# Two of four centring quarters moved from VectorE to GpSimd in the start of a fused transformer block

## The chip, the core and the metric

The kernel runs on one core of a Trainium2 chip. The metric is the device time of one execution in microseconds (us). The time before the change is 691.56 us, the median of 3 runs (691.15 to 691.78).

## What is computed

One pre-norm transformer block over 2048 rows of 1024 columns in bf16: layer norm, sliding-window attention (32 heads of 32 columns, each query sees itself and the 255 keys before it), an output product and a residual, then a second layer norm and a dense part with SiLU, with a second residual. Cut to what matters:

```python
def _layernorm(x, axis=-1, eps=1e-5):
    m = jnp.mean(x, axis=axis, keepdims=True)
    v = jnp.var(x, axis=axis, keepdims=True)
    return (x - m) / jnp.sqrt(v + eps)

x = A_x
h = x + _A_ref(_layernorm(x, axis=-1), A_wqkv, A_wo)
h2 = h + _B_ref(_layernorm(h, axis=-1), B_w1, B_w2)
```

`_A_ref` multiplies by `wqkv` (1024 x 3072), does the windowed softmax attention and multiplies by `wo`. `_B_ref` multiplies by `w1` (1024 x 3584), applies SiLU and multiplies by `w2`.

## The kernel before

The 2048 rows are worked in four blocks of 512 rows, and a block in four row tiles of 128 rows, the number of partitions. For each block the kernel normalises the rows, transposes them (TensorE needs the 1024 columns on the partitions), and forms v, q and k; attention of a block is woven between the products of the next block. The output product and the dense part follow. The scheduling is by hand: every engine runs its instructions in the order in which the program writes them, and semaphores make one engine wait for another.

The change lies in the start, before any of this is in full swing. The very first products (v of row tiles 0 and 1) do not wait for a finished layer norm. Each of the two tiles is only centred, transposed and multiplied; the factor one over the standard deviation is applied to the product later. The order of work for tile j is:

- `half_mean(j, 1, nc.scalar)` (L467): ScalarE sums columns 512 to 1023, scaled by -1/1024, into a column of `mean`. `half_mean(j, 0, nc.vector)` (L469): VectorE does the same for columns 0 to 511, by an instruction that also writes its accumulator.
- `center(j)` (L474): four quarters of 256 columns each, `x_mid = x_ring + mean half + mean half`, bf16 in SBUF to bf16 in SBUF.
- `turn_first(j, h, ...)` (L224, L227): TensorE transposes the two 128-column pieces of quarter h into a PSUM bank, and ScalarE (or VectorE, for the last two quarters of tile 1) copies them to `lnT_b[0]`.
- products (L497) with the first 512 columns of the v weights, accumulated over the eight 128-column pieces of the tile.

TensorE's order is a list written by hand, in which a pair (j, h) is a transposition of quarter h of tile j, and a triple (j, k0, k1) are the products over pieces k0 to k1 - 1:

```python
ORDER = [
    (0, 0), (0, 1), (0, 2), (0, 0, 2), (0, 3), (0, 2, 4), (1, 0), (0, 4, 6), (1, 1), (1, 2), (1, 3), (1, 0, 4),
    (1, 4, 6), (0, 6, 8), (1, 6, 8),
]
```

Ahead of it, TensorE runs a few matmuls on zeros in float32 (`busy`, L173) while the first row tile is on its way from memory. After it come the products of the second half of the v columns (L515), the transposes of row tile 2 (L519) and the rest of v (L249), then q and k (L259).

GpSimd's work in the start is to build the identity matrix for the transposes and to set the ones column of `v` (L167, a memset). Later it does the selects of the attention mask (L382). Its instruction order and that of VectorE are those of the program. The normalisation of whole row tiles in later blocks is one VectorE tensor_scalar over 128x1024 (L208); `norm_first` (L485) is the same for tiles 0 and 1, in place, ahead of their transposition by DMA (L212).

Of the kernel before, what the change touches and what calls it, by code (L numbers as in the profile page):

```python
# [12 lines left out]
ALU = mybir.AluOpType  # L13
# [35 lines left out]
def kernel(  # L49
# [10 lines left out]
    nc = tc.nc  # L60
# [400 lines left out]
    mean = small.tile([P, 6], F32, name="mean")  # L461
# [9 lines left out]
    def center(j):  # L471
        for h in range(4):
            out, in0 = (x[j][:, h * 256:(h + 1) * 256] for x in (x_mid, x_ring))
            nc.vector.tensor_scalar(out=out, in0=in0, scalar1=mean[:, j * 2:j * 2 + 1], scalar2=mean[:, j * 2 + 1:j * 2 + 2], op0=ALU.add, op1=ALU.add)  # L474

    acc_banks += [o[:].rearrange("p a b -> p (a b)") for o in o_ps]
    def var_first(j):
# [9 lines left out]
    for j in range(2):  # L487
        half_mean(j, 1, nc.scalar)
        half_mean(j, 0, nc.vector)
        center(j)  # L490
    nc.vector.tensor_tensor(out=mean[:, 4:6], in0=mean[:, 0:4:2], in1=mean[:, 1:4:2], op=ALU.add)
    first = [next_acc() for _ in range(2)]
    for step in ORDER:
        if len(step) == 3:
            j, k0, k1 = step
# [193 lines left out]
    for b in range(NB):  # L689
# [4 lines left out]
        for ft in range(FT):  # L694
# [8 lines left out]
            if b == 0 and 7 <= ft < 15:  # L703
                j, c = divmod(ft - 7, 2)
# [60 lines left out]
```

## Time and profile before

| What | us |
|---|---|
| median of 3 runs | 691.56 (691.15 to 691.78) |
| span of the profiled execution, first to last instruction | 690.4 |
| busy in the span: TensorE | 676.3 (98%) |
| VectorE | 292.3 (42%) |
| ScalarE | 244.5 (35%) |
| GpSimd | 161.1 (23%) |
| first row tile landed, first half mean starts | 4.03 |
| first transposition | 5.24 |

The profiled execution has no time of its own beside its span; the median of the runs is 1.2 us above the span. In the profile PE is TensorE, PEld its weight loads, DVE is VectorE, ACT is ScalarE, POOL is GpSimd, SP is SyncE, which issues most DMAs. L474 is line 474 of the kernel. A line of the timeline gives start, length, engine, line, operation, output, input, shapes and a count; instructions of one kind that follow each other are merged into one line. A pair of square brackets at the end gives the engine's idle time before it and what ended it. Ends of matmuls are modelled, their starts are recorded.

### The profile page before, as it was taken

Reading aid. Unit: us, or ns where it says so; the run is one execution under the profiler, and the core shown is the slowest. Engines: PE = TensorE matmul, PEld = TensorE weight load, DVE = VectorE, ACT = ScalarE, POOL = GpSimd, SP = SyncE. Lnnn points to the kernel's source line nnn. Section 1 sums busy time; section 2 is a strip of 40 time slices with the busy share of each in tenths; the row PEclk is TensorE's granted clock in tenths of the full one; section 3 lists DMA queues with packets and bytes.
Section 4 is the critical chain, followed back from the end, with each engine's and each line's share of the span. In section 5 each row is a group of like instructions: output and inputs, shape, how many; then the busy total and the mean of one; then the engine's idle time right before and its main releaser. Section 6 shows DMA issues by size and latency. Waiting matters only on the chain.

```text
span 690.4 us, 14117 instructions
## 1 busy us (share of the span) xinstructions
PE 676.3 (98%) x5890; PEld 342.2 (50%) x6004; DVE 292.3 (42%) x613; ACT 244.5 (35%) x466; POOL 161.1 (23%) x295
## 2 busy tenths in 40 slices
PE   8999999999999999999999999999999999999998
PEld 4445555555555555544444444444444444444445
DVE  5167646744444458443316133343133251333111
ACT  6326666666676667421310033300133100233000
POOL 1007666666666656500000000000000000000000
PEclk9999999999999999999999999999999999999999
DMA  7933142137240888970023310022300124100110
GB/s 249 283 40 93 32 74 75 22 62 188 73 131 17 247 257 248 230 266 32 32 85 108 91 39 0 1 91 70 85 0 1 20 92 94 39 1 1 30 39 24
DMA packets 78640, 61.48 MB, mean 89 GB/s; under 512 B 52464, under 2 KB 62704, under 8 KB 78576
## 3 DMA queue, kind: packets, MB, share of 16 engines
q1 hardware_dynamic: 78432, 60.31, 32.2%
q8 instruction: 47, 0.77, 0.5%
q10 hardware_dynamic: 144, 0.26, 0.1%
q14 instruction: 17, 0.14, 0.1%
HBM read 39.85 MB, written 8.39 MB: 70 GB/s over the span
## 4 chain that ended last, share of the span: by engine, by line
PE 97%; issue 1%; DMA 0%; DVE 0%; DVEq 0%
PE hacc L675 19%; PE acc L259 16%; PE hacc L712 14%; PE acc L712 14%; PE acc L675 9%; PE acc L280 7%; PE acc L249 6%; PE o_ps L392 5%; PE sc L312 3%; PE hacc L280 1%; PE sc L364 1%; PE sc L338 1%; PE o_ps L249 1%; DMA r_o<-in_A_x_dram 0%; PE acc L497 0%
## 5 line engine op out<-in xcount | busy, mean ns | idle before, releaser
L382 POOL TENSOR_SCALAR_AFFINE_SELECT r_e<-r_e 128x512 bf16<-128x512 bf16 (+1 forms) x288 | 158.2, 564 | 124.8 <-ACT r_e L372 61.9
L712 PEld LDWEIGHTS <-r_a 128*128 128x128 bf16 x952 | 90.9, 98 | 103.0
L675 PEld LDWEIGHTS <-r_w 128*128 128x128 bf16 x896 | 87.3, 98 | 105.1 <-issue 0.5
L675 PE MATMUL hacc<-r_e,r_w 128*128 128x512 bf16 x468 | 104.9, 379 | 0.5
L712 PE MATMUL hacc<-r_a 128*128 128x512 bf16 (+1 forms) x496 | 100.2, 361 | 0.4
L324 ACT ACTIVATE r_e<-sc 128x768 bf16<-128x768 f32 x96 | 78.2, 814 | 47.9 <-PE sc L312 47.9
L712 PE MATMUL acc<-r_a 128*128 128x512 bf16 (+1 forms) x439 | 94.5, 372 | 0.5
L684 ACT ACTIVATE r_n<-hacc 128x512 f32<-128x512 f32 x30 | 17.9, 597 | 178.9 <-PE hacc L675 177.8
L259 PEld LDWEIGHTS <-r_w 128*128 128x128 bf16 x512 | 47.1, 98 | 55.0 <-issue 1.0
L261 DVE CAST r_a<-acc 128x512 bf16<-128x512 f32 x56 | 38.7, 692 | 57.0 <-PE acc L259 54.4
L259 PE MATMUL acc<-r_t,r_w 128*128 128x512 bf16 x233 | 56.5, 380 | 2.4 <-issue 1.7
L259 PE MATMUL acc<-r_w 128*128 128x512 bf16 x240 | 56.0, 379 | 1.5 <-issue 0.9
L392 PEld LDWEIGHTS <-r_e 128*128 128x128 bf16 x1440 | 47.4, 96 | 17.9
L392 PE MATMUL o_ps<-r_a,r_e 128*128 128x33 bf16 x1440 | 48.1, 178 | 0.0
L280 PE MATMUL acc<-r_o,r_a 128*128 128x512 bf16 x188 | 46.2, 380 | 1.9 <-issue 1.1
L675 PE MATMUL acc<-r_e,r_w 128*128 128x512 bf16 x191 | 43.3, 379 | 0.2
L727 DVE SCALAR_TENSOR_TENSOR r_t<-acc,r_t 128x512 bf16<-128x512 f32 (+1 forms) x16 | 10.6, 665 | 69.3 <-PE acc L712 69.3
L325 ACT ACTIVATE r_e<-sc 128x256 bf16<-128x256 f32 x96 | 37.5, 390 | 0.0
L280 PEld LDWEIGHTS <-r_a 128*128 128x128 bf16 x256 | 23.4, 98 | 26.9
L685 DVE SCALAR_TENSOR_TENSOR r_a<-r_n,hacc 128x512 bf16<-128x512 f32 x30 | 20.6, 688 | 33.0 <-ACT r_n L684 33.0
L685 DVE SCALAR_TENSOR_TENSOR r_a<-r_a,hacc 128x512 bf16<-128x512 f32 x30 | 20.6, 688 | 31.2 <-ACT r_a L684 31.2
L727 DVE SCALAR_TENSOR_TENSOR r_t<-hacc,r_t 128x512 bf16<-128x512 f32 (+1 forms) x18 | 11.6, 647 | 51.2 <-PE hacc L712 51.2
(103 smaller groups left out, 549.2 us busy)
## 6 DMA issues: line engine op xcount, KB each, us to landing
r_w<-in_B_w_dram SPq DMA_DIRECT2D x8, 896.0 KB, 5.2
r_a<-in_B_w_dram SPq DMA_DIRECT2D x7, 1024.0 KB, 7.5
r_w<-in_A_wqkv_dram SPq DMA_DIRECT2D x4, 1024.0 KB, 9.3
h_dram<-r_t SPq DMA_DIRECT2D x16, 256.0 KB, 2.8
r_t<-h_dram SPq DMA_DIRECT2D x16, 256.0 KB, 2.9
out_dram<-r_t SPq DMA_DIRECT2D x31, 128.0 KB, 1.7
r_o<-in_A_x_dram SPq DMA_DIRECT2D x15, 256.0 KB, 4.4
r_e<-h_dram SPq DMA_DIRECT2D x3, 1024.0 KB, 5.8
```

Of the source, the lines that this page charges most:

```text
L249: nc.tensor.matmul(acc, lhsT=lnT_b[b % 2][:, kt, j * P:(j + 1) * P], rhs=wv[:, kt, c * 512:(c + 1) * 512], start=(kt == 0), stop=(kt == KT ...
L259: nc.tensor.matmul(acc, lhsT=wqk[:, kt, col0:col0 + P], rhs=lnT_b[b % 2][:, kt, :], start=(kt == 0), stop=(kt == KT - 1))
L261: copy(out=(qT, kT)[which][b][:, g, :], in_=acc)
L280: nc.tensor.matmul(acc, lhsT=qT[b][:, g, j * P:(j + 1) * P], rhs=wo[:, g, c * 512:(c + 1) * 512], start=(g == 0), stop=(g == G - 1))
L324: nc.scalar.activation(out=tri[:, :, :, 64:256], in_=both, func=ACT.Exp, scale=scale)
L325: nc.scalar.activation(out=e[:, 1024:1280].rearrange("p (h q) -> p h q", q=P), in_=bank[:, :, 192:320], func=ACT.Exp, scale=scale)
L382: nc.gpsimd.affine_select(out=dst, in_=src, pattern=[[0, n] for n in dst.shape[1:-1]] + [[sgn, P]], compare_op=ALU.is_ge if upper else ALU ...
L392: nc.tensor.matmul(o_ps[pair][:, qt * 2 + hh, 0:VW], lhsT=chunk_of(i, bank, piece, pair, hh), rhs=v[:, b * 4 + kt, g * 4 + pair * 2 + hh, ...
L675: nc.tensor.matmul(acc, lhsT=w1[:, kt, ft * P:(ft + 1) * P], rhs=ln2T[b][:, kt, :], start=(kt == 0), stop=(kt == KT - 1))
L685: nc.vector.scalar_tensor_tensor(out=gT[:, ft, :], in0=th, scalar=1.0, in1=acc, op0=ALU.add, op1=ALU.mult)
L712: nc.tensor.matmul(acc[:, 0:c1 - c0], lhsT=gT[:, ft, j * P:(j + 1) * P], rhs=w2[ft // 4][:, ft % 4, c0:c1], start=(ft == 0), stop=(ft == F ...
L727: nc.vector.scalar_tensor_tensor(out=t_out[j % 2][:, c0:c1], in0=acc[:, 0:c1 - c0], scalar=0.5, in1=t_in[j % 2][:, c0:c1], op0=ALU.mult, o ...
```

## The change

The third and fourth quarter of row tile 0 (columns 512 to 1023) are centred by GpSimd instead of VectorE. The other two quarters of tile 0 and all four of tile 1 stay on VectorE, and so does everything else.

```diff
     def center(j):
         for h in range(4):
             out, in0 = (x[j][:, h * 256:(h + 1) * 256] for x in (x_mid, x_ring))
-            nc.vector.tensor_scalar(out=out, in0=in0, scalar1=mean[:, j * 2:j * 2 + 1], scalar2=mean[:, j * 2 + 1:j * 2 + 2], op0=ALU.add, op1=ALU.add)
+            engine = nc.gpsimd if j == 0 and h > 1 else nc.vector
+            engine.tensor_scalar(out=out, in0=in0, scalar1=mean[:, j * 2:j * 2 + 1], scalar2=mean[:, j * 2 + 1:j * 2 + 2], op0=ALU.add, op1=ALU.add)
```

On VectorE the half mean of tile 1 (L469) then follows right behind the second quarter of tile 0. On GpSimd the two quarters stand between the memset of `v` and the first select, behind a wait for the row tile and both half means. TensorE's transposes of quarters 2 and 3 wait for GpSimd instead of VectorE.

## The prediction

> **What bounds the kernel now.** I read the busy times of the page first, then the chain of waits for the first 13 us (the change lies there), then the timeline of single stretches to get single instructions.
>
> Page, parts 1 and 4:
>
> ```profile
> PE 676.3 (98%) x5890; PEld 342.2 (50%) x6004; DVE 292.3 (42%) x613; ACT 244.5 (35%) x466; POOL 161.1 (23%) x295
> PE 97%; issue 1%; DMA 0%; DVE 0%; DVEq 0%
> ```
>
> TensorE is busy for 98% of the span and is 97% of the chain that ended last. Whatever happens to VectorE or GpSimd counts only as far as it moves TensorE. The chain in order of time (start, length, what):
>
> ```profile
> 4.03 0.71 DVE r_e L469 x2
> ...
> 4.84 0.36 DVE r_e L474
> 5.20 0.05 issue
> 5.24 0.91 PE tp L224 x6
> 6.15 0.88 PE acc L497 x2
> 7.03 0.21 PE tp L224 x2
> 7.24 0.85 PE acc L497 x2
> 8.10 0.21 PE tp L224 x2
> 8.31 0.68 PE acc L497 x2
> 8.99 0.33 PE tp L224 x6
> 9.32 1.29 PE o_ps L497 x6
> ```
>
> Up to 5.24 us the chain is VectorE's: half mean of row tile 0, then only its first centring quarter. From there it is TensorE without a hole. So quarters 1 to 3 of tile 0, the mean of tile 1 and the centring of tile 1 are off the path already. The same lines show TensorE's clock: two 512-column matmuls take 0.85 us (0.43 each) at 7.24 and six take 1.29 us (0.215 each) from 9.32. It runs at half rate until some 8.7 us, 3.45 us after 5.24 (the pair at 8.31 takes 0.68, one at each rate).
>
> Timeline of the stretch itself (start, length, engine, line, what, idle before):
>
> ```profile
> 4.56 0.19 ACT L467 ACTIVATION_READ_ACCUMULATOR r_e<-r_o 128x1 f32 x1
> 4.84 1.11 DVE L474 TENSOR_SCALAR r_e<-r_o,mean 128x256 bf16<-128x256 bf16 x4
> 5.24 0.91 PE L224 MATMUL tp<-ident,r_e 128*128 128x128 bf16 x6 [0.77 <-DVE r_e L474]
> 5.86 0.68 DVE L469 TENSOR_SCALAR_CACHE_REDUCE r_e<-r_o 128x512 bf16<-128x512 bf16 x1
> 6.66 1.11 DVE L474 TENSOR_SCALAR r_e<-r_o,mean 128x256 bf16<-128x256 bf16 x4
> 1.31 2.32 POOL L167 MEMSET r_a<- 128x512 bf16 x1
> ```
>
> GpSimd is free from 3.63 us. The quarters start 0.257 us apart on VectorE (4.84, 5.10, 5.35, 5.61), and narrow stretches of the timeline put the transposes that need them at 5.24, 5.49, 5.75 and 6.82. The last was ready at about 6.0, so the fourth quarter has 0.8 us to spare; the third has none that shows. The first product matmul starts at 6.00, held by ScalarE's copy of quarter 0 (5.67 to 5.94).
>
> **The change, part by part.** Program order is unchanged on TensorE; the transposes of quarters 2 and 3 now wait for GpSimd. Added waits elsewhere (the in-place normalisation of tile 0 at 15.55 us, one exponential, one load of x on SP's queue) are for work done by about 6 us: nothing behind them is delayed, so nothing. No DMA is moved.
>
> VectorE loses two quarters, 2 x 0.257 = 0.51 us. The second half mean (L469) and tile 1's centring could start that much earlier. On the path this is worth nothing: TensorE takes tile 1's first transpose at 7.89, behind matmuls that follow each other without a hole, and its quarter was ready at about 7.0. So the gain is nil; what is left is what GpSimd costs.
>
> When GpSimd starts: it waits for both half means, the later being ScalarE's accumulator at 4.75. A select of GpSimd that waited for ScalarE started 0.07 us after it (51.12 to 51.19). That gives 4.82, just ahead of VectorE's first quarter at 4.84.
>
> How long a quarter takes there: the trace has no tensor_scalar on GpSimd. The nearest row is the affine select of the same engine and size, SBUF to SBUF, at 413 ns, back to back every 0.36 us; the farthest is the strided memset at L167, 2320 ns for 512 elements, 1.16 us for 256. I take the select.
>
> Do the two engines hinder each other? Rows of the next block's normalisation show it (VectorE tensor_scalar 128x1024, alone and with selects running):
>
> ```profile
> 47.32 0.54 DVE L208 TENSOR_SCALAR r_o<-r_o,st_a,rs_a 128x1024 bf16<-128x1024 bf16 x1
> 75.70 0.76 DVE L208 TENSOR_SCALAR r_o<-r_o,st_a,rs_a 128x1024 bf16<-128x1024 bf16 x1
> 75.77 0.41 POOL L382 TENSOR_SCALAR_AFFINE_SELECT r_e<-r_e 128x256 bf16<-128x256 bf16 x1
> 76.13 0.59 POOL L382 TENSOR_SCALAR_AFFINE_SELECT r_e<-r_e 128x256 bf16<-128x256 bf16 x1
> 133.58 0.99 DVE L208 TENSOR_SCALAR r_o<-r_o,st_a,rs_a 128x1024 bf16<-128x1024 bf16 x1
> 133.66 0.64 POOL L382 TENSOR_SCALAR_AFFINE_SELECT r_e<-r_e 128x512 bf16<-128x512 bf16 x1 [0.57 <-ACT r_e L324]
> ```
>
> A select that starts 0.07 us after VectorE's instruction runs undisturbed (0.41) and VectorE takes 0.22 longer; the next one is itself held up by 0.18. The longer select of 0.64 costs VectorE 0.45. So they take turns, and GpSimd gets in first even when it starts slightly later. From 75.70: delay of VectorE = 0.15 + (start of GpSimd - start of VectorE), not below nothing.
>
> Quarter 0 (VectorE 4.84, GpSimd 4.82): 0.15 - 0.02 = 0.13 late, so the first transpose at 5.37. Quarter 1: VectorE issues it at 5.10 + 0.13 = 5.23; GpSimd's second quarter starts at 4.82 + 0.36 = 5.18, delay 0.15 - 0.05 = 0.10. It is 0.23 late in all, its transposes at 5.72. Quarter 2 is ready on GpSimd by 5.23 and no longer waits for VectorE: its two transposes follow at 5.72 + 2 x 0.107 = 5.94 (half-rate pace of 128 columns, from 0.43 for 512) and end their turn at 6.15. The first product matmul is then at 6.15 instead of 6.00: TensorE loses **0.16 us**. Quarter 3 is ready at about 5.6, needed at 7.0.
>
> If GpSimd holds the way longer than the select does by e, quarter 0 pays e and quarter 1 pays it twice: loss 0.16 + 2e. [...] With the memset's rate e = (4.53 - 0.9) x 256 = 0.93 us (0.9 ns an element from 413 and 640 ns of the two sizes of select), and the loss is 2.0. The lower end: if GpSimd starts 0.1 us later, VectorE's quarter 0 goes first and the loss is about 0. Below nothing it can't go, since the matmul at 6.00 hangs on quarter 0 and ScalarE.
>
> What a loss d before 8.7 us costs at the end: half-rate time is lost. If the clock turns at the same moment, the missing work is done later at double pace, d/2; if the turn moves by d too, d. All later work hangs on TensorE, with no slack that takes it up. Sum: 0.08 to 0.16 us at the value taken, up to 0.4 with e = 0.13. I forecast **+0.2 us**. The profiled execution spans 690.4 us, and the median of the runs is 691.56; I take the 1.2 us around the span as unchanged. That gives a span of 690.6 and a time of **691.8 us**. About 0.2% (1.4 us) is what a measurement of this kernel can tell from no change, so this is "same".
>
> **The rivals.** *The clock turns a whole stretch later (slower).* TensorE was busy with its first matmuls from 1.12 to 4.48 and stayed at half rate; after 0.77 us of idling, 3.45 us of unbroken work raised it. If a new hole at 5.35 to 5.75 spoils this stretch, another such stretch passes at half rate: it costs (3.45 + 0.16) / 2 = 1.8 us, 693.4 us. It decides as soon as the holes exceed what the rise tolerates; the idle 0.77 did not pass, the present 0.1 us between pairs of transposes does. Against it: my holes sum to some 0.3 us, spread out. [...] Chance 0.23.
>
> *GpSimd is slow at this operation (slower).* With the memset's rate, quarter 0 is 0.13 + 0.93 late and TensorE loses 2.0 us. Nothing raises the clock earlier, since work starts later: +1.0 to 2.0, up to 693.6 us. It ends slower from e = 0.6 us. For it: no row shows this operation; against it: the memset's elements lie 66 bytes apart, the quarters' are adjacent. Chance 0.11.
>
> *The freed VectorE pays (faster).* Were a wait of TensorE hidden in the chain, the whole of its idle time between 5.25 and 16 us, 0.14 us by the windows, bounds the gain: 691.4 us, which is still "same". Faster by 1.4 us would need the clock to rise earlier, and its stretch starts no earlier. Chance of that 0.06.
>
> *VectorE isn't freed at all*, its tile-1 mean starting no earlier as it waits its turn: it has 0.9 us to spare there, so the time is the forecast's, 691.8.
>
> **How the numbers follow.** Forecast (loss 0 to 0.5 us, with the harmless rivals) 0.60; slower 0.23 + 0.11 = 0.34; faster 0.06. The range runs from 691.1 (no loss, low end of the runs shown) to 693.6 (both slower rivals' prices); the forecast's own range is 691.1 to 692.3.
>
> **What would show it.** In the profile after: two POOL instructions at about 4.82 and 5.18, near 0.41 us each; VectorE's quarter 0 lengthened from 0.35 to about 0.48; the first transpose at about 5.37; the second L469 at about 5.6; the first L497 matmul near 6.15; matmuls 0.215 apart from about 8.8. Right up to the clock but wrong in the time: matmuls still 0.43 apart after 9.5. Wrong on GpSimd's price: POOL rows of over 0.7 us and the first transpose past 5.7. Wrong altogether: a span that differs by more than this, with nothing of it to be seen by 14 us.

## The result, and the profile after

The changed kernel takes 692.50 us, the median of 21 runs (691.00 to 693.29). The kernel before, run beside it, takes 690.78 us (21 runs, 690.39 to 691.78). The ratio is 1.0018, 95% interval [1.0012, 1.0023]: slower by 0.8 to 1.6 us. That is about the 0.2% that the prediction took as the limit of what can be told, and the interval excludes no change at all. The median lies inside the whole range (691.1 to 693.6) and just above the forecast's own (up to 692.3). The 21 times fall into two groups with nothing between them: nine from 691.00 to 691.43 and twelve from 692.30 to 693.29.

The profiled execution after spans 689.6 us and took 691.43 us, so it belongs to the first group. Its chain of waits in order of time (start, length, what):

```profile
0.81 2.51 DMA r_o<-in_A_x_dram
...
3.34 0.70 DVE r_e L469 x2
4.04 0.03 POOLq L475
4.07 0.14 issue
4.21 2.51 POOL r_e L475 x2
6.72 0.05 issue
6.77 0.28 PE tp L224 x2
7.05 0.43 PE acc L498 x2
```

Before, the chain passed from VectorE's first quarter to TensorE at 5.24 us and stayed there. Now GpSimd's two quarters stand in it for 2.51 us, and TensorE enters only with the transposes of the fourth quarter. (The row tile landed 0.69 us earlier in this execution than in the profile before; times below are therefore counted from the start of the first half mean.) Some lines of the timeline of the same stretch:

```profile
4.16 0.76 DVE L475 TENSOR_SCALAR r_e<-r_o,mean 128x256 bf16<-128x256 bf16 x2
4.21 2.50 POOL L475 TENSOR_SCALAR r_e<-r_o,mean 128x256 bf16<-128x256 bf16 x2 [0.59 <-ACT r_e L467]
4.56 0.70 PE L224 MATMUL tp<-ident,r_e 128*128 128x128 bf16 x4 [0.21 <-DVE r_e L475]
4.84 0.67 DVE L469 TENSOR_SCALAR_CACHE_REDUCE r_e<-r_o 128x512 bf16<-128x512 bf16 x1
5.56 0.28 PE L224 MATMUL tp<-ident,r_e 128*128 128x128 bf16 x2 [0.31 <-POOL r_e L475]
5.69 0.59 PE L498 MATMUL acc<-r_w 128*128 128x512 bf16 x2
6.77 0.28 PE L224 MATMUL tp<-ident,r_e 128*128 128x128 bf16 x2 [0.49 <-POOL r_e L475]
```

One quarter on GpSimd takes 1.25 us (half of the 2.50 for two), where the prediction had 0.41. TensorE waits for both: 0.31 and 0.49 us (the brackets). VectorE does get to tile 1's half mean early: 1.50 us after the first half mean started (4.84 - 3.34), against 1.83 before (5.86 - 4.03). And the two matmuls at 5.69 take 0.59 us together, against 1.03 for the pair at 6.00 before: the clock was already at full rate in this execution. The trace's own clock records put the rise to full rate at 4.08 us here, and at 8.68 us in the profile before. (They begin with the first rise: before it the PEclk column shows 1.00 although the matmuls run at half pace, so a start is judged by the lengths of its matmuls or by the record of the rise.)

### The profile page after: what moved, and what is told of

It is laid out like the page before. It is cut to its first block, busy times and chain, and to the rows that moved or that the text cites. A ratio compares the mean times of both kernels' runs of the same rounds, so it can differ in the third digit from the quotient of the medians.

```text
span 689.6 us, 14232 instructions
## 1 busy us (share of the span) xinstructions
PE 684.5 (99%) x6004; PEld 341.5 (50%) x6004; DVE 292.0 (42%) x611; ACT 244.4 (35%) x466; POOL 163.0 (24%) x297
## 4 chain that ended last, share of the span: by engine, by line
PE 98%; DMA 1%; POOL 0%; DVE 0%; SPq 0%; issue 0%; POOLq 0%
PE hacc L676 20%; PE acc L259 17%; PE hacc L713 14%; PE acc L713 14%; PE acc L676 9%; PE acc L249 7%; PE acc L280 6%; PE o_ps L392 5%; PE sc L312 2%; PE hacc L280 2%; PE sc L364 1%; PE sc L338 1%; DMA r_a<-r_a 1%; PE o_ps L249 1%; DMA r_o<-in_A_x_dram 0%; POOL r_e L475 0%
## 5 line engine op out<-in xcount | busy, mean ns | idle before, releaser
L259 PE MATMUL acc<-r_t,r_w 128*128 128x512 bf16 x256 | 59.6, 380 | 0.0
L259 PE MATMUL acc<-r_w 128*128 128x512 bf16 x256 | 57.8, 380 | 0.0
L280 PE MATMUL acc<-r_o,r_a 128*128 128x512 bf16 x208 | 48.7, 380 | 0.0
```

What stands on the lines that cost most here:

```text
L259: nc.tensor.matmul(acc, lhsT=wqk[:, kt, col0:col0 + P], rhs=lnT_b[b % 2][:, kt, :], start=(kt == 0), stop=(kt == KT - 1))
L280: nc.tensor.matmul(acc, lhsT=qT[b][:, g, j * P:(j + 1) * P], rhs=wo[:, g, c * 512:(c + 1) * 512], start=(g == 0), stop=(g == G - 1))
```

## The experiments

Each run has a time series and one profile. One number from the profile is used throughout, called "the start stage" here: the time from the first half mean of tile 0 (first L469 instruction) to the first matmul of the second half of the v columns (L515 before), which comes right after all products of the first half. It leaves out when x landed and everything later. It is 7.29 us in the profile before (11.32 - 4.03) and 7.02 in the first profile after (10.36 - 3.34): with an early rise the changed kernel is even shorter here than the kernel before with a late one, so profiles are compared below only with the moment of the rise beside them.

**The two kernels again.** No edit.

> The kernel before, unchanged, for the spread of its times and a second look at when TensorE's clock rises. Price theory (GpSimd's two quarters take 1.2 to 1.3 us each and TensorE waits for both): median 690.8 us. Clock theory (the clock rises when a stretch of some 3.4 us was busy enough, the stretches lie differently in every run, and the waits for GpSimd push the rise back in some runs): also 690.8, single runs 690.4 to 691.8, and the half-rate matmuls end at another moment than 8.7 us.

> The changed kernel, unchanged. Price theory: each run 0.4 to 0.8 us over the kernel before, one group of times near 691.4. Clock theory: two groups again, 691.0 to 691.5 and 692.3 to 693.3, by when the clock rises.

Measured: the kernel before 691.55 us (11 runs, 690.84 to 692.38; ratio to the other runs of it 1.0004 [0.9996, 1.0013]), the changed one 692.16 (691.11 to 693.22; 1.0013 [1.0002, 1.0024]). This time the changed kernel's times don't fall into two groups: 691.67, 691.68, 692.15 and 692.16 lie between. Its profile fell on a time of 693.22, the longest of the eleven:

```profile
4.74 0.81 PE L224 MATMUL tp<-ident,r_e 128*128 128x128 bf16 x4 [0.27 <-DVE r_e L475]
5.74 0.40 PE L224 MATMUL tp<-ident,r_e 128*128 128x128 bf16 x2 [0.20 <-POOL r_e L475]
5.93 1.06 PE L498 MATMUL acc<-r_w 128*128 128x512 bf16 x2
6.94 0.40 PE L224 MATMUL tp<-ident,r_e 128*128 128x128 bf16 x2
...
9.05 0.85 PE L224 MATMUL tp<-ident,r_e 128*128 128x128 bf16 x6
```

Same program, other clock: matmul pairs take 1.06 us, and six transposes at 9.05 still 0.85 where 0.50 is full rate. From the lengths of the matmuls, and by the clock records (10.07), the clock rose at about 10.1 us here, against 4.08 in the first profile of the same kernel. One profile from each end suggests that long times are late rises and short ones early rises; it doesn't show it for every run. At half rate the wait for the third quarter is 0.20 us, and for the fourth none is left: the slow matmuls ahead of it fill the time. The copy of the kernel before had its rise at about 8.8 us. The start stage is 7.38 us there (11.37 - 3.99) and 8.52 here (12.04 - 3.52).

**Only the fourth quarter on GpSimd.**

```diff
-            engine = nc.gpsimd if j == 0 and h > 1 else nc.vector
+            engine = nc.gpsimd if j == 0 and h > 2 else nc.vector
```

> Only the fourth quarter of tile 0 on GpSimd; the third is back on VectorE. Price theory: the quarter is ready about 1.4 us after the half means, TensorE needs it about 1.5 us after them, so no wait or one below 0.2 us: 690.6 to 691.0 us. Clock theory: no new hole, so no second group of times, 690.8. Contention theory (VectorE's own quarters get longer beside GpSimd and that is the cost): one or two quarters 0.15 us longer, +0.2 us, 691.0.

Measured: 691.26 us (11 runs, 690.34 to 693.39), ratio 1.000 [0.999, 1.001]. GpSimd's price is the same, but nobody waits:

```profile
4.45 1.29 POOL L475 TENSOR_SCALAR r_e<-r_o,mean 128x256 bf16<-128x256 bf16 x1 [0.83 <-ACT r_e L467]
```

It ends at 5.74; the transposes of that quarter run at 6.28, behind two matmuls, with no wait in front. The price theory holds; the pure contention theory, with its +0.2 us, can't be told from nothing by this interval. The times reach 693.39 without a second group set apart, so such long times come without any wait for GpSimd too.

**The same two quarters on GpSimd as well, for nobody.** VectorE centres all four quarters as before; GpSimd repeats two of them into unused memory.

```diff
+    def center_too():
+        for h in range(2, 4):
+            nc.gpsimd.tensor_scalar(out=view(r_e, 5120 + 256 * h, 256), in0=x_ring[0][:, h * 256:(h + 1) * 256], scalar1=mean[:, 0:1], scalar2=mean[:, 1:2], op0=ALU.add, op1=ALU.add)
...
         center(j)
+        if j == 0:
+            center_too()
```

> The kernel before, with GpSimd centring the same two quarters as well, into memory that nobody reads. Price and clock theory: nobody waits for GpSimd, 690.8 us. Contention theory: VectorE's four quarters are lengthened beside it, and the time goes to where the changed kernel is, 692.0 or more.

Measured: 691.83 us (11 runs, 690.46 to 693.28), ratio 1.0007 [0.9994, 1.0019], which tells nothing apart. The profile does:

```profile
4.59 1.43 DVE L474 TENSOR_SCALAR r_e<-r_o,mean 128x256 bf16<-128x256 bf16 x4
4.66 2.51 POOL L478 TENSOR_SCALAR r_e<-r_o,mean 128x256 bf16<-128x256 bf16 x2 [1.03 <-ACT r_e L467]
5.00 1.07 PE L224 MATMUL tp<-ident,r_e 128*128 128x128 bf16 x6 [0.52 <-DVE r_e L474]
9.48 1.75 PE L503 MATMUL o_ps<-r_w 128*128 128x512 bf16 x6
```

Four VectorE quarters take 1.43 us beside GpSimd and 1.11 alone: the contention is 0.32 us over two GpSimd instructions, 0.16 each, not the length of the instruction. TensorE waits for nothing on GpSimd, and yet its clock rose only at about 10.1 us (six matmuls at 9.48 still take 1.75 us, 1.46 at full rate). The start stage is 8.14 us (11.93 - 3.79).

**The clock held up from the start, first try.** TensorE runs 30 units of 128 columns on zeros in place of 7; the loads of x wait for the first 14, because a copy of their result is written into the buffers that the loads fill.

```diff
+    for n in (4, 4, 4, 2):
+        busy(n)
+    for j in range(2):
+        nc.vector.tensor_copy(out=x_ring[j][:, 0:8], in_=o_ps[0][:, 0, 0:8])
+    for n in (4, 4, 4, 4):
+        busy(n, 1)
+
     load_x(0, 0)
...
-    for n in (4, 3):
-        busy(n)
```

> The kernel before with its start held back: 14 + 16 units of 128 columns of matmuls on zeros in place of 7, the first loads of x waiting for the first 14, so that TensorE's clock is up in every run before the first transposition. All theories: about 5 to 8 us longer than the kernel before, one group of times; it is the partner of the next two.

> The changed kernel with the same held-back start. Price theory: 0.6 to 0.9 us over its partner with the held-back start, from two waits for GpSimd at full clock, in one group of times. Clock theory: the difference shrinks to the waits themselves, and the 1.7 us between the medians of the plain pair doesn't appear; no second group. Contention theory: 0.3 us.

> Only the fourth quarter on GpSimd, with the held-back start. Price theory: within 0.2 us of the partner with all quarters on VectorE, perhaps below it, since tile 1's centring starts 0.26 us earlier. Contention theory: 0.2 us above it.

Measured: 700.79, 700.64 and 700.84 us (4 runs each). The medians say nothing about the change, since the partner lost its clock in three of its four runs, the profiled one among them, and the changed kernel in three of four (mean granted clock 0.997 or 0.998 in place of 1.000). Stretches of the kernel before with the held-back start (stretch, its length, busy time and count of PE, PEld, DVE, ACT, POOL, then PEclk, DMA share, GB/s):

```profile
10.00:13.40 3.40, 1.44 (x10) 0.51 (x9) 1.98 (x7) 2.01 (x7) 0.00 (x0) 1.00 1.06 368
13.50:16.80 3.30, 3.30 (x17) 1.83 (x15) 1.72 (x8) 1.56 (x6) 0.00 (x0) 0.50 1.08 363
17.00:20.00 3.00, 3.00 (x16) 1.35 (x15) 2.15 (x7) 2.62 (x7) 0.00 (x0) 1.00 1.10 350
```

TensorE was busy for 1.44 of 3.4 us around its idle time, and the next 3.4 us ran at half rate (PEclk 0.50), though fully busy. The kernel with one quarter on GpSimd fell back as well, after 2.05 us. The changed kernel idled just as long, 1.94 us, but stayed at full rate; what decided is not shown. (Stretches of 3.41 us, the length of the half-rate stretch recorded in the kernel before from 13.47 to 16.88, laid around the idle time from the recorded rise, have TensorE busy for 1.46 us in the kernel before, 1.30 with one quarter moved and 1.48 in the changed kernel, almost alike.) That profile gives the changed kernel's start stage at full rate: 7.01 us (17.50 - 10.49).

**The clock held up, second try.** 16 + 21 units, so that the idle time is short (the edit is shown against the first try).

```diff
-    for n in (4, 4, 4, 2):
+    for n in (4, 4, 4, 4):
         busy(n)
...
-    for n in (4, 4, 4, 4):
+    for n in (4, 4, 4, 4, 4, 1):
         busy(n, 1)
```

> The held-back start again, kernel before, now with 16 + 21 units of matmuls on zeros, so that TensorE idles less than 0.5 us ahead of the first transposition (it idled 1.96 us in the first try, and its clock fell back to half rate). All theories: full rate through the whole start, one group of times.

> The changed kernel with that start. Price theory: at full rate TensorE waits for both quarters of GpSimd (0.31 and 0.49 us in the profile after), so 0.5 to 0.8 us over its partner, and no more. Clock theory: the same, since no rise is left to be moved; the part of the plain pair's difference that goes beyond it was the clock. Contention theory: 0.15 to 0.3 us.

Measured: 699.11 us before (4 runs, 698.61 to 700.13), 700.96 after (4 runs, 700.55 to 701.42). Both profiles are at full rate throughout the start; the idle time was 0.9 and 1.0 us, not the 0.5 aimed at, and was borne. Some lines of the kernel before, then of the changed one:

```profile
12.88 0.80 PE L227 MATMUL tp<-ident,r_e 128*128 128x128 bf16 x6 [0.88 <-DVE r_e L477]
13.53 0.60 PE L500 MATMUL acc<-r_w 128*128 128x512 bf16 x2
13.97 0.28 PE L227 MATMUL tp<-ident,r_e 128*128 128x128 bf16 x2
14.08 0.59 PE L500 MATMUL acc<-r_w 128*128 128x512 bf16 x2
14.70 0.11 PEld L227 LDWEIGHTS <-r_e 128*128 128x128 bf16 x2 [0.52 <-DVE r_e L477]
14.71 0.28 PE L227 MATMUL tp<-ident,r_e 128*128 128x128 bf16 x2
...
17.75 1.03 PE L518 MATMUL o_ps<-r_w 128*128 128x512 bf16 x4
```

```profile
13.35 0.70 PE L227 MATMUL tp<-ident,r_e 128*128 128x128 bf16 x4 [1.01 <-DVE r_e L478]
14.35 0.28 PE L227 MATMUL tp<-ident,r_e 128*128 128x128 bf16 x2 [0.31 <-POOL r_e L478]
14.47 0.59 PE L501 MATMUL acc<-r_w 128*128 128x512 bf16 x2
15.55 0.28 PE L227 MATMUL tp<-ident,r_e 128*128 128x128 bf16 x2 [0.48 <-POOL r_e L478]
...
19.14 1.03 PE L519 MATMUL o_ps<-r_w 128*128 128x512 bf16 x4
```

The first half means start at 11.67 and 12.14, so the start stage is 6.08 us with all quarters on VectorE and 7.00 with two on GpSimd: **0.92 us at full rate**, a little above what was expected. The three full-rate profiles of the changed kernel agree (7.02, 7.01 and 7.00; in the first the clock rose at 4.08 us, ahead of the first transposition); of the kernel before there is one. The waits are 0.31 and 0.48 us again, but they are not the terms of the difference. The transposes of the fourth quarter come 3.41 us after the half mean (15.55 - 12.14) against 2.30 (13.97 - 11.67), 1.11 us later, because GpSimd's two quarters last until 3.36. Of that, 0.18 comes back at tile 1: the kernel before has to wait there for VectorE, whose quarter, started at 14.30, holds the transposes until 14.71, while the two matmuls at 14.08, 0.215 each, would have let them start at 14.51. The medians differ by 1.85 us; with four runs each and x landing at different times (0.47 us apart in these profiles) they can't be read more closely, and the profile's 0.92 is the better number.

**GpSimd's price list.** Extra instructions beside an otherwise unchanged kernel.

```diff
+    for n in (128, 256, 512, 1024):
+        nc.gpsimd.tensor_scalar(out=dst[:, 0:n], in0=src[:, 0:n], scalar1=m0, scalar2=m1, op0=ALU.add, op1=ALU.add)
...
+        nc.gpsimd.tensor_copy(out=dst[:, 0:n], in_=src[:, 0:n])
```

> The kernel before with ten extra GpSimd instructions into memory that is written again before it is read, at about 4 to 40 us: tensor_scalar with two scalars from memory at 128, 256, 512 and 1024 columns, with one scalar from memory, with a constant, and copies, at 256 and 1024. If the price is by the element (as the memset's 4.5 ns): 0.6, 1.2, 2.4 and 4.7 us. If it is mostly a fixed price: 1.1 to 1.2 us at 128 and below 2 us at 1024. If the second scalar costs it, one scalar or a constant falls to about 0.4 us at 256.

Groups of instructions of POOL by form (line, shapes, count, busy us, mean ns, idle before; 128 columns left out): L581 has two scalars from memory, L583 one, L585 a constant, L587 is the copy.

```profile
L581 POOL TENSOR_SCALAR r_e<-r_e,mean 128x1024 bf16<-128x1024 bf16 x1 | 3.8, 3777 | 0.1
L583 POOL TENSOR_SCALAR r_e<-r_e,mean 128x1024 bf16<-128x1024 bf16 x1 | 2.8, 2837 | 0.1
L585 POOL TENSOR_SCALAR r_e<-r_e 128x1024 bf16<-128x1024 bf16 x1 | 2.8, 2812 | 0.1
L581 POOL TENSOR_SCALAR r_e<-r_e,mean 128x512 bf16<-128x512 bf16 x1 | 2.1, 2098 | 0.1
L581 POOL TENSOR_SCALAR r_e<-r_e,mean 128x256 bf16<-128x256 bf16 x1 | 1.2, 1212 | 0.1
L585 POOL TENSOR_SCALAR r_e<-r_e 128x256 bf16<-128x256 bf16 x1 | 1.1, 1090 | 0.1
L587 POOL COPY r_e<-r_e 128x1024 bf16<-128x1024 bf16 x1 | 1.0, 1040 | 0.1
L587 POOL COPY r_e<-r_e 128x256 bf16<-128x256 bf16 x1 | 0.4, 396 | 0.1
```

The price goes by the element: 3.3 ns each between 256 and 1024 columns with two additions ((3777 - 1212) / 768), 2.2 with one, 0.84 for a copy. One addition costs the same with a scalar from memory (2837 ns) as with a constant (2812), and is still nearly three times a copy: in these rows doing arithmetic is dear, not where the scalar comes from. The instructions started at 5 us, at once with the start's own work, and the kernel's time (694.18 us, one run) is not comparable.

**One more unit of filling ahead of the first transposition.**

```diff
-    for n in (4, 3):
+    for n in (4, 4):
         busy(n)
```

> The kernel before with one more unit of 128 columns on zeros ahead of the first transposition (8 in place of 7), so that TensorE's idle stretch there is some 0.25 us in place of 0.75. Clock theory: more stretches of 3.4 us are busy enough, the clock rises earlier in about a third of the runs: median 0.2 to 0.5 us below the kernel before, fewer runs above 691.5. Price theory has no say. Rival: the extra unit ends after the first quarter is ready when x lands early, and costs 0.2 us: 691.2.

> The same longer filling with only the fourth quarter on GpSimd. Price theory: as with the longer filling alone, within 0.2 us, since nobody waits for that quarter; slightly faster if tile 1's centring was late at full rate.

Measured: 691.20 us with all quarters on VectorE, ratio 1.0001 [0.999, 1.0011], and 690.97 with the fourth on GpSimd, 0.9999 [0.9989, 1.0009]. No gain: the expectation missed. In the profile of the first, the clock had risen by 7.6 us (the matmuls at 7.57 run at full pace), but TensorE waited for weights just ahead of that:

```profile
PE acc L497 <- DMA r_w<-in_A_wqkv_dram: 0.6, 1, 0.6
```

This is one line of the waits from 5.1 to 20 us (waited in total, times, longest). In this execution, then, the gain of an earlier clock was eaten by loads that hadn't landed. In the profile of the second, the clock rose at 5.90 us, no load was late, and the start stage was 6.09 us (9.93 - 3.84), against 6.08 with all quarters on VectorE at full rate from its beginning. Its first six transposes still ran at half rate, but tile 1 did not wait for VectorE (the matmuls at 6.46, the transposes 0.43 behind them at 6.89). At full rate throughout, moving the fourth quarter alone may thus save up to the 0.08 us by which tile 1's half mean starts earlier (1.75 us after the first against 1.83); that is an estimate, and the times tell neither a cost nor a gain. No version here beats the kernel before.

## Why the prediction came out as it did

The time, its whole range and the bound ("same") held, in part by luck. The forecast was +0.2 us, the two medians are 1.7 apart and the interval starts at 0.8. It began from 691.56 us, the median of three runs, where 21 runs have 690.78, and the range reached as far as 692.50 only by the prices of the slower rivals. The steps under it held only in part.

- *What bounds the start*: right for the half-rate start it was read from. TensorE takes the work as it comes, and VectorE's freed time is worth nothing there. At full rate it isn't quite so: TensorE, in the kernel before, waits 0.2 us for tile 1's first quarter. With both quarters moved, tile 1's half mean starts 0.33 us earlier (1.50 against 1.83 after the first); with only the fourth moved 0.08 (5.33 - 3.58 = 1.75), since GpSimd holds VectorE up meanwhile (VectorE's three quarters take 1.01 us there, against 0.86 for three without GpSimd).
- *GpSimd's duration*: wrong, and the mis-sized term. The select at 0.41 us was taken because it has the engine, the size and the memory in common. It only keeps or replaces its elements, and a copy costs the same as it (0.40 us); a tensor_scalar takes 1.21 to 1.29. The far bound, the memset's 1.16 us, came closest, though the quarters do not share its stride, which was the reason against it. Of the prediction's two signs for a wrong price, the POOL rows over 0.7 us came and the late first transposition did not.
- *VectorE blocked by GpSimd*: the wrong way of losing. The sum put the whole loss into VectorE's first two quarters, which would wait for a part of each GpSimd instruction (0.13 and 0.10 us) and for all of the excess if it were longer (0.16 + 2e). The first was not touched (0.35 us, the first transposition 1.22 us after the half mean, as before), the second was 0.15 us longer (0.50), and in the run where GpSimd worked for nobody it is 0.16 for each GpSimd instruction. The e = 0.13 behind the sum's upper end of 0.4 is shown by no run: beside GpSimd instructions of 1.25 us, 0.84 longer than the select, VectorE lost 0.15 to 0.16 for each.
- *The loss at TensorE*: 0.16 us was forecast. At half rate the first product matmul came 2.41 us after the half mean against 1.97, a loss of 0.44 us, all from the third quarter, which the prediction had ready early. At full rate the stage is 0.92 us longer, because the fourth quarter, forecast with more than a microsecond to spare, is late as well: TensorE still waits 0.48 us for it after its wait for the third.
- *What half-rate time costs*: the rule of half (a rise later by d costs d/2) held as far as it can be worked out. The repeat of the kernel before and the run where GpSimd worked for nobody, neither of which waits for GpSimd, rose 4.82 and 6.27 us after the half mean; half of the difference is 0.73, and their start stages differ by 0.76. The profiles of the two kernels again differ by 1.14 us in the start stage; their rises lie 4.82 and 6.55 us after the half mean, which is worth 0.87. What is left, 0.27 us, is an estimate of the change's price with a late rise, close to the +0.2 forecast. Beside the run where GpSimd worked for nobody (8.14 us, rise at 6.27) the same sum leaves 0.24. The profile of before was an execution with a late rise, and the forecast was made for it alone.
- *When the clock rises*: not as forecast. The forecast took the rise at 8.7 us, as in the one profile it was read from. It came at 4.08 and 5.90 us and before 7.6 in some profiles and at 8.68, 8.81 and 10.1 in others, the late ones also of kernels without the waits. Half-rate stretches whose fall and rise are both recorded took 3.41 us (13.47 to 16.88 us in the held-back start, 7.92 to 11.33 in the price list's run). That a busy enough stretch of some 3.4 us raises the clock, the clock theory of the expectations, was the author's supposition; what raises it is not shown.
- *The rivals*: "GpSimd is slow" is what happened, by another way and with its price at 0.3 to 0.9 us and not 1 to 2: TensorE waits for GpSimd's own quarters, while VectorE's, which the rival had late, are hardly touched. "The clock turns a whole stretch later" is seen in single executions, but not shown to be the change's doing.

The price of 0.3 us (late rise, estimated) to 0.92 us (early rise, shown) lies within the second interval of the plain pair, 0.1 to 1.7 us; only its upper end lies in the first, 0.8 to 1.6. So a part of the measured difference, up to 1.3 us (1.6 - 0.3), may come from how often the clock is late, and whether the waits make it late more often stays open. For it: twelve of 21 times after lie above 692 us, where none of the 21 before does, and seven of eleven against ten of 44 in the repeat. Against it: the changed kernel's times are shifted by its price anyway, and five of eleven are above 692 in the run where nobody waits for GpSimd, whose profile rose at 10.1 us too. Three of the changed kernel's 32 executions, all of 692.9 us or more, have a mean granted clock of 0.998, like the held-back starts that fell back; one execution of the kernel before has it too, of 693.93 us. Telling it would take the moment of the rise in many executions, not their times.

## What to carry to other kernels

Before moving an elementwise step to GpSimd, find a row of GpSimd with the same arithmetic, not only the same size: a select or copy of 256 columns took 0.40 us, a tensor_scalar 1.25, against VectorE's 0.26 from one quarter to the next. Ask for each moved piece when its reader needs it: the fourth quarter moved alone kept nobody waiting, the third did, and it made the fourth late as well. And where the first microseconds run on a clock that may still have to rise (here it did so between 4.08 and 10.1 us), read a start from more than one profile, counting from an event of the work itself, since one profile shows only one of the cases.

## What the runs showed of the hardware that was not expected

- A GpSimd tensor_scalar holds VectorE up far less than its length: 0.15 to 0.16 us per instruction of 1.25 us. An affine select of the profile before, 0.41 us long, held it up for 0.22 (0.54 to 0.76): in these rows the one that does more arithmetic is the lighter neighbour.
- A start at the same place in the program ran at full rate, at half rate, or fell from full to half and rose again 3.41 us later (13.5 to 16.9 us in the held-back start). An idle time of 1.9 to 2.1 us lost the clock in two of three profiles, one of 0.9 to 1.0 in neither of two.
- x's first tile landed anywhere between 3.34 and 4.03 us with the same first instructions, as much as the change itself is worth.
